# A new plan for the first part of a packed-attention, gated-unit and leaky-ReLU kernel

## The chip, the core and the metric

The kernel runs on one core of a Trainium2 chip. The metric is the time of one execution on the device in microseconds, as the median of several runs. One more execution was taken with the hardware profiler; every row shown here is from that one.

## The reference, cut to what matters

```
p_packed = sm_attn(p, k, v)            # 8 batches x 8 heads: 32 packed queries over 576 keys, head dim 64
out      = sm_attn(q, p_packed, p_packed)        # 576 queries over the 32 packed keys
x = out.transpose(0, 2, 1, 3).reshape(4608, 512)
x = (sigmoid(x @ w_gate) * (x @ w_val)) @ w_out          # w_gate, w_val: 512 x 1536
h = x @ w_in                                             # 512 x 2048
return max(0.01 * h, h) @ w_out2
```

The weights arrive as float64 in pairs of 32-bit words, and the kernel itself turns them into float32.

## The kernel before, in words

There are two parts. The **first part** runs batch by batch (b = 0 to 7). Of each batch it computes the two attentions and then the gated products for 12 blocks f of 128 columns, and stores each block in DRAM (`g1d`). Beside this it converts the weights. The **second part** multiplies by the three remaining weight matrices (line 851) in blocks of 768 tokens, with fewer products by a scheme of sums and differences. It begins when the last gated block is stored.

A `Plan` writes the order of the work out before anything runs on the chip. Every task has an engine (PE, ACT, DVE, POOL or DMA), a cost in us, a rank, tasks that it comes after, and buffers that it takes from named pools and gives back. `Plan.run` steps through a list schedule: whenever an engine is free in the plan, the ready task of lowest rank whose buffers are free is placed next on that engine. On the chip every engine then takes its instructions in that order and waits on semaphores. A task that the plan thinks ready and that isn't holds up all that stands behind it on its engine. A result counts as there 0.1 us after its task, a load 2.2 us after.

The tasks of the first part:

- **Weight units** (`unit`): a load of 512 KB on the SP queue into one of four `raw64` buffers, two ACT passes (lines 227, 234), two DVE passes (lines 238, 242), one addition on POOL (line 249). There are 24 units for gate and value weights (`unit_gv`, four for each of six column groups i, ranks -60 + 4i and up). There are 44 more for the later weights (`staged`, ranks from 900), which are then combined on POOL (line 310), split (ACT line 316, POOL line 322) and stored in DRAM from POOL's queue (line 330).
- **Attention** (`attention(b)`, base rank 100 (b - 1)): loads of k, p, v and q; transposes of k (DVE lines 410 to 416); first scores (`scores1`, PE line 427, both head groups G in one task); row maximum (`max1`), exponential (`exp1`), normalisation, a transposition on PE (`flip`, line 482) and its copy (`unflip`), the product with v (`pv`, line 503), the packing (`pack1` to `pack3`); then transposes of q, second scores (line 427), softmax on DVE in four steps around `exp2` (ACT line 547), and the split of the result into the high and low operands Ah and Al (`fin`, ACT line 578 and DVE line 580). The two halves h of the second attention are tasks of their own, as are the two groups G of the first.
- **Combinations** (`m_mm`, PE line 658): for each i the packed rows times the gate and value weights, then split by ACT (line 672, `mh`) and DVE (line 675, `ml`).
- **Gated products** (`mm`, PE line 691): for each f two tasks of 12 matmuls, gate and value; a sigmoid on ACT (`gate`, line 701), a multiplication on DVE (`times`, line 707) and a store on the SP queue.

PSUM holds four tiles. The plan has them as two pools: `pair` with two for the gated products, and `misc` with two for everything else. Batch 0's loads have ranks -100 to -56.5, in front of and among the first gate and value units; batch 1's have ranks from 0, behind all of them. Combinations have ranks 100 b + 16 i - 95, sigmoids and multiplications 100 b + 8 f - 90.

Of the kernel before, what the change touches and what calls it, by code (L numbers as in the profile page):

```python
# [29 lines left out]
class Plan:  # L30
# [7 lines left out]
    LAG = {"DMA": 2.2}  # L38

    def __init__(self):  # L40
        self.tasks, self.pools, self.holders = [], {}, {}
# [4 lines left out]
    def add(self, engine, us, rank, fn, after=(), take=(), give=()):  # L46
        i = len(self.tasks)
        self.tasks.append((engine, us, rank, fn, [a for a in after if a is not None], take, give))
        for name in dict.fromkeys(name for name, _ in take):
            self.pools[name][1].append(i)  # L50
        for key in give:
            self.holders[key] = self.holders.get(key, 0) + 1
        return i

    def run(self):
# [12 lines left out]
        while len(order) < n:  # L68
            for e, heap in ready.items():
# [3 lines left out]
                while heap:  # L73
# [3 lines left out]
                    if all(  # L77
# [9 lines left out]
                        us = self.tasks[i][1]  # L87
# [4 lines left out]
                        heapq.heappush(events, (now + us + self.LAG.get(e, 0.1), i))  # L92
# [12 lines left out]
            while events and events[0][0] <= now:  # L105
                _, i = heapq.heappop(events)
                if i < 0:
                    continue
                for j in next_of[i]:
# [23 lines left out]
def pack_attention_glu_lrelu(  # L133
# [83 lines left out]
    def unit(key, rank, load, target, after=(), give=(), loads=1):  # L217
# [148 lines left out]

    def attention(b):
        st = {}
# [52 lines left out]
        def scores(ps, w, key, half):  # L421

            for e in range(2):
                for j in range(NJ):
                    for G in range(2):
# [9 lines left out]
        def scores1():  # L435
            ps = st["sk"] = [ps_pair() for _ in range(2)]
            for half in range(2):
                scores(lambda G, j: ps[G][rows(G, j), half, :HS], pt, "k", half)
# [7 lines left out]
        def max1(G):  # L446
            def fn():
                mx = small("mx", [P, 1])
                nc.vector.tensor_reduce(out=mx, in_=st["sk"][G][:, :, :HS], axis=AX.XY, op=ALU.max)
# [4 lines left out]
        def exp1(G):  # L454
            def fn():
                a, sm = big(), small("sm", [P, 1])
                nc.scalar.activation(
                    a.rearrange("p (x y) -> p x y", x=2), st["sk"][G][:, :, :HS], AF.Exp,
# [110 lines left out]
        def fin(half, part):  # L569
            def fn():  # L570
# [14 lines left out]
        ld = r0 if b else -100  # L585
        Lk = [add("DMA", 1.8, ld + G, load_qk(k, "k", G), take=[K("qk", "k", G)]) for G in range(2)]
        Lp = add("DMA", 0.7, ld + 0.5, load_p, take=[K("praw")])
        Lv = add("DMA", 3.6, ld + 2 if b else -58.5, load_v, take=[K("v")])
        Lq = [add("DMA", 1.8, (ld + 3 if b else -57.5) + G, load_qk(q, "q", G), take=[K("qk", "q", G)])
              for G in range(2)]  # L590
        tp = add("DVE", 0.25, r0, p_t, [Lp] + ([packed[b - 1, "ck"]] if b else []), give=[K("praw")[1]])
        tk = [
            add("DVE", 0.75, r0 + 0.1 * j, tr("k", j), [Lk[j // 2]], take=[K("w576", "tk", j)],
                give=[K("qk", "k", j // 2)[1]])
            for j in range(NJ)
        ]
        ck = add("PE", 2.3, r0 + 1, scores1, [tp, *tk], take=[K("misc", "sk", 0), K("misc", "sk", 1)],
                 give=[K("w576", "tk", j)[1] for j in range(NJ)])
        packed[b, "ck"] = ck
        ex, fl, un = [], [], []  # L600
        for G in range(2):
            m = add("DVE", 0.95, r0 + 2 + G, max1(G), [ck])
            ex.append(add("ACT", 0.9, r0 + 2 + G, exp1(G), [m], take=[K("w576", "a", G)],
                          give=[K("misc", "sk", G)[1]]))
        for G in range(2):
            nm = add("DVE", 0.2, r0 + 4 + G, norm1(G), [ex[G]])
            nm = add("ACT", act(576), r0 + 4 + G, scale1(G), [nm])
            fl.append(add("PE", 0.7, r0 + 4 + G, flip(G), [nm], take=[K("misc", "f", G)],
                          give=[K("w576", "a", G)[1]]))
            un.append(add("ACT", 1.0, r0 + 5 + G, unflip(G), [fl[G]], take=[K("aT", G)],  # L610
                          give=[K("misc", "f", G)[1]]))
        pvt = add("PE", 2.1, r0 + 7, pv, [*un, Lv], take=[K("misc", "pp")],
                  give=[K("aT", 0)[1], K("aT", 1)[1], K("v")[1]])
        p1 = add("DVE", 0.5, r0 + 7, pack1, [pvt])
        p2 = add("PE", 0.2, r0 + 7, pack2, [p1])
        p3 = add("DVE", 0.25, r0 + 7, pack3, [p2], take=[K("pps")], give=[K("misc", "pp")[1]])
        packed[b] = p3
        tq = [
            add("DVE", 0.75, r0 + 8 + 0.1 * j, tr("q", j), [Lq[j // 2]], take=[K("w576", "tq", j)],
# [3 lines left out]
        last = []  # L623
        for h in range(2):
            c = add("PE", 1.2, r0 + 9 + h, scores2(h), [p3, *tq], take=[K("misc", "sq", h)],
                    give=[K("w576", "tq", j)[1] for j in range(NJ)])
            a = add("DVE", 0.8, r0 + 9 + h, soft2a(h), [c], take=[K("w576", "t", h)],
                    give=[K("misc", "sq", h)[1]])
            a = add("DVE", 1.7, r0 + 9 + h, soft2b(h), [a])
            last.append(add("ACT", 0.8, r0 + 9 + h, exp2(h), [a]))  # L630
        begin = add("", 0, r0 + 9, lambda: None, take=[K("A")])
        fins = []
        for h in range(2):
            a = add("DVE", 1.7, r0 + 11 + h, soft2c(h), [last[h]])
            a = add("DVE", 0.8, r0 + 11 + h, soft2d(h), [a], take=[K("w576", "u", h)],
                    give=[K("w576", "t", h)[1]])
            a = add("ACT", act(576), r0 + 11 + h, fin(h, 0), [a, begin])
            fins.append(add("DVE", dve(576), r0 + 11 + h, fin(h, 1), [a],
                            give=[K("w576", "u", h)[1]]))
        ready_a[b] = fins  # L640

# [3 lines left out]
    def gated(b, units):  # L645
# [70 lines left out]
        for i in range(NF1 // 2):  # L716
            m = add("PE", 1.2, r0 + 16 * i - 95, m_mm(i), [packed[b], *units[i]], take=[K("misc", i), K("mhl", i)],
                    give=[("pps", b)])
            h = add("ACT", act(1024), r0 + 16 * i - 95, m_split(i, 0), [m])
            l = add("DVE", dve(1024), r0 + 16 * i - 95, m_split(i, 1), [h], give=[K("misc", i)[1]])  # L720
            for f in (2 * i, 2 * i + 1):
                r = r0 + 8 * f
                g = add("PE", 1.6, r, mm(f, 0), [l, *ready_a[b]], take=[K("pair", f, 0)])
                vv = add("PE", 1.6, r + 1, mm(f, 1), [g], take=[K("pair", f, 1)],
                         give=[K("mhl", i)[1]] + ([("A", b)] if f == NF1 - 1 else []))
                s = add("ACT", act(576), r - 90, gate(f), [g], take=[K("sg", f)], give=[K("pair", f, 0)[1]])
                if b == B - 1 and f == NF1 - 1:
                    x = add("DVE", dve(576), r - 90, lambda: (times(NF1 - 1)(), store(NF1 - 1)()),
                            [s, vv], give=[K("pair", f, 1)[1], K("sg", f)[1]])
                    g1_done[b].append(x)  # L730
                    glu_end[b] = x
                else:
                    x = add("DVE", dve(576), r - 90, times(f), [s, vv], give=[K("pair", f, 1)[1]])
                    g1_done[b].append(add("DMA", 0.95, r - 90, store(f), [x], give=[K("sg", f)[1]]))
# [310 lines left out]
    with tc.manual_schedule():  # L1045
# [6 lines left out]
        attention(0)  # L1052
        for b in range(B):
            if b + 1 < B:
                attention(b + 1)
            gated(b, units)
# [40 lines left out]
```

## Time and profile before

| what | us |
|---|---|
| median of 3 runs (1528.1 to 1539.04) | 1528.98 |
| the profiled execution's own time | 1533.33 |
| its span, first to last instruction | 1531.6 |
| last gated matmul ends, first matmul of line 851 at full flow | 554.8 and 559.8 |

PE is TensorE's matmuls, PEld its weight loads, DVE VectorE, ACT ScalarE, POOL GpSimd, SP the engine whose queue issues most loads and stores (SPq). In the tables of stretches each engine's busy time stands with its instructions in brackets, then the mean granted TensorE clock as a share of full speed, the mean busy share of the DMA engines and what they moved. In lists of waits the columns are the time in total, how often, and the longest.

### The profile page before, as it was taken

The page shows a single profiled execution, that of the slowest core. Times are in us where ns is not written, and L with a number is a line of the kernel's source. Part 1 is how long each engine was busy: PE and PEld are TensorE (multiplying, and loading weights), DVE is VectorE, ACT ScalarE, POOL GpSimd, SP SyncE. Part 2 cuts the span into 40 slices and gives each one's busy share as a digit, 9 for nine tenths or more (in the row PEclk, how much of TensorE's full clock was granted, in tenths as well). Part 3 has the DMA queues.
Part 4 walks back from the last instruction along what each step waited for, and adds up shares of the span by engine and source line. Part 5 has one row for each costly group of instructions (what it writes and reads, how often), then busy time and mean ns, then how long its engine had stood idle before and what let it go on. Part 6 is the DMA issues. An engine that isn't in the chain of part 4 may idle for free.

```text
span 1531.6 us, 26682 instructions
## 1 busy us (share of the span) xinstructions
PE 1424.7 (93%) x10368; PEld 1335.4 (87%) x10368; DVE 1066.6 (70%) x1350; ACT 763.9 (50%) x1015; POOL 491.6 (32%) x571
## 2 busy tenths in 40 slices
PE   4586889889889989999999999999999999999997
PEld 1464767778767889999999999999999999999997
DVE  4788787889886447578467856686558854985483
ACT  4476766767666334454245434544355434543450
POOL 1347486396767201003510250026001620040002
PEclk8698999999989999999999999999999999999999
DMA  9997888788875739888988898889988998897886
GB/s 223 227 275 237 287 262 308 251 268 296 283 250 208 283 104 336 295 252 274 351 297 255 262 367 292 254 264 328 333 252 264 285 359 270 253 298 250 253 253 179
DMA packets 150829, 414.92 MB, mean 271 GB/s; under 512 B 32800, under 2 KB 43504, under 8 KB 150704
## 3 DMA queue, kind: packets, MB, share of 16 engines
q1 hardware_dynamic: 121056, 335.71, 69.5%
q0 software_dynamic: 26208, 77.09, 14.3%
q8 instruction: 83, 1.36, 0.3%
q10 hardware_dynamic: 3440, 0.42, 0.2%
q14 instruction: 42, 0.34, 0.1%
HBM read 335.02 MB, written 78.12 MB: 270 GB/s over the span
## 4 chain that ended last, share of the span: by engine, by line
PE 80%; DMA 8%; DVE 4%; ACT 4%; issue 2%; SPq 1%; POOL 1%; POOLq 0%; ACTq 0%; DVEq 0%
PE ps_pair L851 62%; PE ps_pair L691 14%; DMA raw<-in_moe_w_gate_dram 2%; PE ps_pair L658 2%; DMA raw<-in_moe_w_in_dram 1%; DMA raw<-in_moe_w_val_dram 1%; PE ps_pair L427 1%; DMA wd<-HL 1%; DVE ml L675 1%; ACT L701 1%; DMA raw<-in_moe_w_out_dram 1%; DVE Y L242 1%; DVE sg L707 1%; PE ps_pair L503 1%; ACT mh L672 0%
## 5 line engine op out<-in xcount | busy, mean ns | idle before, releaser
L851 PE MATMUL ps_pair<-op,wu 128*128 128x384 f32 x5544 | 964.0, 337 | 4.3 <-ACT op L794 4.0
L851 PEld LDWEIGHTS ps_pair<-op,wu 128*128 128x128 f32 x5544 | 963.0, 188 | 5.2 <-ACT op L794 4.2
L1031 POOL DMA_DIRECT2D out_dram<-os x225 | 132.3, 596 | 628.6 <-DVE os L1013 537.3
L794 ACT CAST op<-rawg 128x768 fp32r<-128x768 f32 x168 | 137.7, 835 | 211.9 <-DVE rawg L785 104.4
L691 PE MATMUL ps_pair<-Ah,ml 128*128 128x288 f32 x768 | 180.6, 317 | 55.6 <-ACT Ah L578 24.9
L691 PEld LDWEIGHTS ps_pair<-Ah,ml 128*128 128x128 f32 x768 | 127.0, 197 | 104.3 <-ACT sg L701 30.4
L799 DVE TENSOR_TENSOR op<-rawg,op 128x768 fp32r<-128x768 f32 x168 | 158.3, 952 | 75.4 <-ACT op L794 74.0
L868 DVE TENSOR_TENSOR tmp<-ps_pair,tmp 128x768 f32<-128x768 f32 x72 | 68.9, 957 | 152.9 <-PE ps_pair L851 104.4
L691 PE MATMUL ps_pair<-Al,mh 128*128 128x288 f32 x768 | 170.2, 303 | 1.1 <-DVE Al L580 1.1
L691 PE MATMUL ps_pair<-Ah,mh 128*128 128x288 f32 x768 | 169.1, 302 | 0.0
L794 ACT CAST op<-G 128x768 fp32r<-128x768 f32 x168 | 134.6, 834 | 59.9 <-PE ps_pair L851 44.8
L799 DVE TENSOR_TENSOR op<-G,op 128x768 fp32r<-128x768 f32 x168 | 156.0, 951 | 7.7 <-ACT op L794 7.3
L924 POOL DMA_DIRECT2D rawg<-g1d x96 | 68.7, 719 | 208.0 <-DVE op L799 95.1
L691 PEld LDWEIGHTS ps_pair<-Al,mh 128*128 128x128 f32 x768 | 128.9, 197 | 1.8 <-DVE Al L580 1.8
L691 PEld LDWEIGHTS ps_pair<-Ah,mh 128*128 128x128 f32 x768 | 128.1, 196 | 0.0
L987 ACT ACTIVATE G<-G 128x768 f32<-128x768 f32 x96 | 81.2, 846 | 59.1 <-DVE G L984 58.1
L322 POOL TENSOR_TENSOR HL<-Y,HL 128x1024 fp32r<-128x1024 f32 (+1 forms) x44 | 94.3, 2147 | 43.1 <-ACT HL L316 42.9
L701 ACT ACTIVATE sg<-ps_pair 128x576 f32<-128x576 f32 x96 | 62.4, 650 | 83.0 <-PE ps_pair L691 77.7
L862 ACT COPY tmp<-ps_pair 128x768 f32<-128x768 f32 x72 | 57.7, 802 | 91.0 <-PE ps_pair L851 90.5
L707 DVE TENSOR_TENSOR sg<-sg,ps_pair 128x576 f32<-128x576 f32 x96 | 71.3, 743 | 42.6 <-ACT sg L701 17.8
L785 DVE TENSOR_TENSOR rawg<-rawg 128x768 f32<-128x768 f32 x96 | 90.3, 954 | 5.2 <-DMA rawg<-g1d 2.9
L785 DVE TENSOR_TENSOR G<-G 128x768 f32<-128x768 f32 x96 | 91.4, 953 | 0.3
(78 smaller groups left out, 1196.0 us busy)
## 6 DMA issues: line engine op xcount, KB each, us to landing
wu<-wu SPq DMA_DIRECT2D x168, 512.0 KB, 4.7
wu<-wd SPq DMA_DIRECT2D x168, 512.0 KB, 4.5
wu<-wp SPq DMA_DIRECT2D x126, 512.0 KB, 4.8
g1d<-sg SPq DMA_DIRECT2D x96, 288.0 KB, 4.0
rawg<-g1d POOLq DMA_DIRECT2D x48, 384.0 KB, 8.0
raw<-in_moe_w_out_dram SPq DMA_DIRECT2D x28, 512.0 KB, 5.3
raw<-in_k_dram SPq DMA_DIRECT2D x16, 576.0 KB, 5.6
raw<-in_q_dram SPq DMA_DIRECT2D x16, 576.0 KB, 5.6
```

Source lines behind the costliest of these rows:

```text
L322: nc.gpsimd.tensor_tensor(out=hl[:, :, 1], in0=t["y"][:, x0:x1], in1=hl[:, :, 0].bitcast(F32), op=ALU.subtract,)
L691: nc.tensor.matmul(ps[:, t, :HS], w, x[:, t * HS:(t + 1) * HS], start=(n == 0), stop=(n == len(pairs) - 1),)
L701: nc.scalar.activation(st["sg", f], st["gv", f, 0][:, :, :HS], AF.Sigmoid)
L707: nc.vector.tensor_tensor(out=sg, in0=sg, in1=st["gv", f, 1][:, :, :HS], op=ALU.mult)
L785: nc.vector.tensor_tensor(out=src(g, o), in0=src(g, a), in1=src(g, b), op=ALU.subtract)
L794: nc.scalar.copy(h, src(g, c))
L799: (nc.gpsimd if on_pool(i, g) else nc.vector).tensor_tensor(out=l, in0=src(g, c), in1=tiles["op", st, i, g][0].bitcast(F32), op=ALU.subtract)
L851: nc.tensor.matmul(ps[c][:, m, :TB], a, x[:, kk, :], start=(fresh and kk == 0 and y == 0), stop=(end and kk == 1 and y == 2), skip_group_c ...
L868: nc.vector.tensor_tensor(out=T[x], in0=ps[c][:, :, :TB], in1=T[y], op=ALU.add)
L924: nc.gpsimd.dma_start(out=t[:, :, t0 - base:t0 - base + m], in_=g1d[b][:, f:f + 2, s0:s0 + m])
L987: nc.scalar.activation(dest(), dest(), AF.Prelu, alpha=0.01)
L1031: queues[turn % len(queues)].dma_start(out=ob[:, s0:s0 + m, d0:d0 + 32], in_=tiles["os", c][32 * y:32 * y + 32, x, t0:t0 + m],)
```

## The change: what it does

- **The planner.** A task on another engine counts as ready 0.5 us after what it waits for (`SLACK`; 0.2 us for tasks of attention, added by `late`), on the same engine at once. A load counts as there 3.5 us after its cost. ACT's tasks can name a function table, and a switch of table costs 1.5 us in the plan.
- **Costs.** Loads of weight units 1.7 becomes 2.15 us (gate and value) or 1.8; the DVE passes 0.6 and 0.78 become 0.45 and 0.7 (gate and value) or 0.85 and 0.9; loads of batches 0 and 1 become 2.5 (k, q) and 5.5 (v).
- **PSUM.** The pools `pair` and `misc` become one pool `ps` of four.
- **Ranks.** Batch 1's k and p load at -55, v at -49, q at -39, among the gate and value units. Attention's first half has base r0 - 60 (r0 - 80 for batch 0), its middle r0 - 30; batch 1's r0 is 20 lower. Sigmoids and multiplications go from -90 to -100, combinations from -95 to -60, `exp2` to r0 - 100.
- **Tasks.** `scores1` is one task for each G. Both `exp1` are one ACT task, and so are both `exp2`; the pair comes after both of what either needs. The tasks are added in another order (`attention` yields three times).

```diff
-    LAG = {"DMA": 2.2}
+    SLACK = 0.5
...
-                        us = self.tasks[i][1]
+                        us, table = self.tasks[i][1], self.tasks[i][7]
+                        if table and table != self.table:
+                            self.table, us = table, us + 1.5
...
-                        heapq.heappush(events, (now + us + self.LAG.get(e, 0.1), i))
+                        heapq.heappush(events, (now + us + (3.5 if e == "DMA" else 0), i))
...
-                        heapq.heappush(ready[self.tasks[j][0]], (self.tasks[j][2], j))
+                        wait = 0 if self.tasks[j][0] == self.tasks[i][0] else self.tasks[j][8]
+                        heapq.heappush(events, (now + wait, n + j))
...
-        L = add("DMA", 1.7, rank, do_load, take=[("raw64", ("raw64", key))])
+        L = add("DMA", 2.15 if rank < 0 else 1.8, rank, do_load, take=[("raw64", ("raw64", key))])
...
-        s = add("DVE", 0.6, rank, shift, [a])
-        s = add("DVE", 0.78, rank, sign, [s], give=[("raw64", key)])
+        s = add("DVE", 0.45 if rank < 0 else 0.85, rank, shift, [a])
+        s = add("DVE", 0.7 if rank < 0 else 0.9, rank, sign, [s], give=[("raw64", key)])
...
-                    ("A", 2), ("pps", 2), ("pair", 2), ("mhl", 2), ("sg", 3)):
+                    ("A", 2), ("pps", 2), ("mhl", 2), ("sg", 3)):
...
-    plan.pool("misc", 2, loose=True)
+    plan.pool("ps", 4, loose=True)
...
+    def late(engine, *args, **more):
+        return add(engine, *args, slack=0.2, **more)
...
-        ld = r0 if b else -100
+        r1 = r0 - (60 if b else 80)
+        ld = (-100, -55)[b] if b < 2 else r1
...
+        for G in range(2):
+            ck.append(late(
+                "PE", 1.15, r1 + 1 + G, scores1(G), [tp, *tk[2 * G:2 * G + 2]], take=[K("ps", "sk", G)],
+                give=[K("w576", "tk", 2 * G + e)[1] for e in range(2)],
+            ))
+            mx.append(late("DVE", 0.95, r1 + 2 + G, max1(G), [ck[G]]))
...
+        ex = late("ACT", 1.5, r1, lambda: (exp1(0)(), exp1(1)()), mx,
+                  take=[K("w576", "a", G) for G in range(2)],
+                  give=[K("ps", "sk", G)[1] for G in range(2)], table="exp")
+        yield
+        r0 -= 20 * (b == 1)
...
+        Lv = add("DMA", 5.5 if b < 2 else 4.5, (-58.5, -49)[b] if b < 2 else r1 + 2, load_v, take=[K("v")])
+        Lq = [add("DMA", 2.5 if b < 2 else 2.0, ((-57.5, -39)[b] if b < 2 else r1 + 3) + G, load_qk(q, "q", G), take=[K("qk", "q", G)])
...
-            last.append(add("ACT", 0.8, r0 + 9 + h, exp2(h), [a]))
+        ex = late("ACT", 1.5, r0 - 100, lambda: (exp2(0)(), exp2(1)()), sb, table="exp")
...
-            m = add("PE", 1.2, r0 + 16 * i - 95, m_mm(i), [packed[b], *units[i]], take=[K("misc", i), K("mhl", i)],
+            m = add("PE", 1.2, r0 + 16 * i - 60, m_mm(i), [packed[b], *units[i]], take=[K("ps", i), K("mhl", i)],
...
-                s = add("ACT", act(576), r - 90, gate(f), [g], take=[K("sg", f)], give=[K("pair", f, 0)[1]])
+                s = add("ACT", act(576), r - 100, gate(f), [g], take=[K("sg", f)], give=[K("ps", f, 0)[1]],
+                        table="sigmoid")
```

## Rows read from the trace of the kernel before

**Rows 1.** Busy time of each engine by stretches of the first part.

```profile
0.00:50.00 50.00, 17.39 (x236) 7.33 (x236) 27.32 (x55) 19.92 (x35) 7.09 (x11) 0.75 1.03 223
50.00:100.00 50.00, 38.03 (x308) 31.07 (x309) 36.60 (x63) 29.80 (x47) 24.43 (x18) 0.81 0.97 260
100.00:150.00 50.00, 35.03 (x421) 27.89 (x422) 45.36 (x67) 32.68 (x48) 30.16 (x26) 0.86 0.75 240
150.00:500.00 350.00, 315.75 (x3413) 258.12 (x3412) 282.86 (x413) 237.20 (x333) 233.85 (x204) 0.96 0.81 268
500.00:555.00 55.00, 54.53 (x452) 48.03 (x450) 21.31 (x26) 15.87 (x21) 8.02 (x12) 1.00 0.59 213
```

**Rows 2.** The gated matmuls (line 691) alone, PE and PEld, over that part.

```profile
0.00:555.00 555.00, 345.57 (x2304) 323.50 (x2304) 0.92 0.81 255
```

**Rows 3.** The chain that ended last, in order of time: start, length, what.

```profile
35.19 9.31 DMA raw<-in_moe_w_gate_dram
...
519.78 1.02 PE ps_pair L658 x16
520.80 6.54 PE ps_pair L691 x48
```

**Rows 4.** Two of the page's costliest groups: second part's matmuls, sigmoids.

```profile
L851 PE MATMUL ps_pair<-op,wu 128*128 128x384 f32 x5544 | 964.0, 337 | 4.3 <-ACT op L794 4.0
...
L701 ACT ACTIVATE sg<-ps_pair 128x576 f32<-128x576 f32 x96 | 62.4, 650 | 83.0 <-PE ps_pair L691 77.7
```

**Rows 5.** Who waited for whom, 0 to 100 us.

```profile
ACT wc L227 <- DMA raw<-in_moe_w_gate_dram: 28.4, 10, 9.2
...
PE ps_pair L691 <- ACT Ah L578: 13.5, 1, 13.5
...
ACT wc L227 <- DMA raw<-in_moe_w_val_dram: 12.7, 7, 3.7
```

**Rows 6.** PE's waits, 100 to 150 us.

```profile
PE ps_pair L691 <- ACT Ah L578: 11.4, 2, 7.2
```

**Rows 7.** PE's waits, 150 to 500 us.

```profile
PE ps_pair L691 <- ACT sg L701: 10.3, 7, 4.2
PE ps_pair L691 <- DVE ml L675: 6.8, 5, 3.0
PE ps_pair L482 <- ACT w L474: 6.4, 5, 2.1
```

**Rows 8.** SP's queue in order of time, 0 to 140 us.

```profile
44.87 3.25 SPq L381 DMA_DIRECT2D raw<-in_q_dram  x2
...
84.08 2.61 SPq L266 DMA_DIRECT2D raw<-in_moe_w_gate_dram  x4
...
89.20 1.84 SPq L266 DMA_DIRECT2D raw<-in_moe_w_val_dram  x2
```

**Rows 9.** ACT's instructions in order of time, 0 to 145 us.

```profile
48.63 1.33 ACT L578 CAST Ah<-w 128x576 fp32r<-128x576 f32 x2 [2.81 <-DVE w L565]
...
98.67 0.67 ACT L227 ACTIVATE wc<-raw 128x512 f32<-128x512 f32 x1
```

**Rows 10.** DVE's instructions in order of time, 0 to 145 us.

```profile
49.48 1.42 DVE L580 TENSOR_TENSOR Al<-w,Ah 128x576 fp32r<-128x576 f32 x2
...
103.93 2.75 DVE L410 STREAM_TRANSPOSE w<-raw 128x576 f32<-128x576 f32 x4
...
131.99 3.58 DVE L580 TENSOR_TENSOR Al<-w,Ah 128x576 fp32r<-128x576 f32 x1
...
138.04 1.79 DVE L580 TENSOR_TENSOR Al<-w,Ah 128x576 fp32r<-128x576 f32 x1
```

**Rows 11.** POOL's instructions in order of time, from two stretches.

```profile
132.62 2.33 POOL L322 TENSOR_TENSOR HL<-Y,HL 128x1024 fp32r<-128x1024 f32 x1
...
489.83 0.77 POOL L330 DMA_DIRECT2D wd<-HL  x1 [0.30 <-POOL HL L322]
```

**Rows 12.** Loads of the sigmoid's table on ACT, whole first part.

```profile
L701 ACT ACT_TABLE_LOAD x22 | 28.2, 1283 | 0.4
```

More of the change, by code (lines that the diff above doesn't have):

```diff
@@ L30, with add @@
 class Plan:
-    LAG = {"DMA": 2.2}
+    SLACK = 0.5
     def __init__(self):
-        self.tasks, self.pools, self.holders = [], {}, {}
+        self.tasks, self.pools, self.holders, self.table = [], {}, {}, None
     def pool(self, name, n, loose=False):
         self.pools[name] = [n, [], 0, loose]
-    def add(self, engine, us, rank, fn, after=(), take=(), give=()):
+    def add(self, engine, us, rank, fn, after=(), take=(), give=(), table=None, slack=None):
         i = len(self.tasks)
-        self.tasks.append((engine, us, rank, fn, [a for a in after if a is not None], take, give))
+        self.tasks.append((engine, us, rank, fn, list(after), take, give, table,
+                           slack or self.SLACK))
         for name in dict.fromkeys(name for name, _ in take):
@@ L108, in run @@
                     continue
+                if i >= n:
+                    j = i - n
+                    heapq.heappush(ready[self.tasks[j][0]], (self.tasks[j][2], j))
+                    continue
                 for j in next_of[i]:
@@ L419, in tr, with scores @@
             return fn
-        def scores(ps, w, key, half):
+        def scores(ps, w, key, half, groups=(0, 1)):
             for e in range(2):
                 for j in range(NJ):
-                    for G in range(2):
+                    for G in groups:
                         r = slice(32 * j, 32 * j + 32)
@@ L433, in scores, with scores1, fn @@
                         )
[L435 to L438, printed above, removed]
+        def scores1(G):
+            def fn():
+                ps = st["sk", G] = ps_pair()
+                for half in range(2):
+                    scores(lambda g, j: ps[rows(g, j), half, :HS], pt, "k", half, (G,))
+            return fn
         def scores2(half):
@@ new lines, in attention @@
+        yield
+        r0 -= 20 * (b == 1)
+        fl, un = [], []
+        for G in range(2):
+            nm = late("DVE", 0.3, r0 - 30 + G, norm1(G), [ex])
+            nm = late("ACT", 0.8, r0 - 30 + G, scale1(G), [nm])
+            fl.append(late("PE", 0.8, r0 - 30 + G, flip(G), [nm], take=[K("ps", "f", G)],
+                          give=[K("w576", "a", G)[1]]))
+            un.append(late("ACT", 0.9, r0 - 29 + G, unflip(G), [fl[G]], take=[K("aT", G)],
+                          give=[K("ps", "f", G)[1]]))
@@ L613, in attention @@
+        Lv = add("DMA", 5.5 if b < 2 else 4.5, (-58.5, -49)[b] if b < 2 else r1 + 2, load_v, take=[K("v")])
+        Lq = [add("DMA", 2.5 if b < 2 else 2.0, ((-57.5, -39)[b] if b < 2 else r1 + 3) + G, load_qk(q, "q", G), take=[K("qk", "q", G)])
+              for G in range(2)]
+        pvt = late("PE", 2.1, r0 - 27, pv, [*un, Lv], take=[K("ps", "pp")],
                   give=[K("aT", 0)[1], K("aT", 1)[1], K("v")[1]])
-        p1 = add("DVE", 0.5, r0 + 7, pack1, [pvt])
-        p2 = add("PE", 0.2, r0 + 7, pack2, [p1])
@@ L732, in gated @@
                 else:
[L733 to L734 removed]
+                    x = add("DVE", dve(576), r - 100, times(f), [s, vv], give=[K("ps", f, 1)[1]])
+                    g1_done[b].append(add("DMA", 0.95, r - 100, store(f), [x], give=[K("sg", f)[1]]))
     NWU, NOP = 6, 22
@@ L1051, in pack_attention_glu_lrelu @@
         units = [[unit_gv(i, g, jh) for g in range(2) for jh in range(2)] for i in range(NF1 // 2)]
[L1052 to L1056, printed above, removed]
+        steps = [attention(b) for b in range(B)]
+        for b in range(B + 1):
+            if b < B:
+                next(steps[b])
+            if b:
+                next(steps[b - 1])
+            if b < B:
+                next(steps[b])
+            if b:
+                gated(b - 1, units)
         rank = 900.0
```

65 lines of the change are left out of this document (27 added, 38 removed).

## The prediction

> **What bounds the kernel now.** I read the table of stretches first, because the change touches only what happens before the last gated block is stored. In the first 555 us PE stands idle for 94 (each stretch less its busy time): 32.6 in the first 50 us, 12.0 in the next, 15.0 in the third, 34.2 from 150 to 500, and then half a microsecond [rows 1]. In the same stretches the granted clock is 0.75, 0.81, 0.86, 0.96 and 1.00: wherever PE had stood idle, part of its work then ran at the lower of its two levels, 1.2 instead of 2.4 GHz. The cost shows in the gated matmuls: 2304 of them took 345.6 us [rows 2], while 48 at full speed take 6.54 [rows 3], which makes 314 for all. So the low clock costs a further 31 us there. Idle time and low clock together are the 125 us that a plan can win back in the first part; no engine's amount of work changes.
>
> The last 55 us are plain matmul, 54.5 of 55 busy, so the first part ends where PE's queue ends, and a microsecond taken out of an earlier idle stretch moves that end, as long as the weights are ready. They have slack: POOL issues its last store of converted weights at 489.8 [rows 11], 65 us ahead. The other engines are no tighter than PE: from 150 to 500 us DVE is busy 283 of 350, ACT 237, POOL 234, DMA 0.81 [rows 1]. DVE at 81% is the nearest rival. The second part is matmul throughout: 5544 matmuls with 4.3 us of idle time in front of all of them [rows 4].
>
> Then the lists of waits, to see what the idle time is. In the first 100 us ACT stands 41.1 us at the head of its queue for gate and value weights (28.4 + 12.7) [rows 5], with attention's work behind it; the chain of waits agrees, with a gate load of 9.3 us in it [rows 3]. DMA is saturated there, share 1.03 and 0.97 at 223 and 260 GB/s [rows 1]. PE waits 13.5 us for batch 0's Ah [rows 5] and then 11.4 for batch 1's [rows 6]. Later the waits are short and many: sigmoids 10.3, the split of the combinations 6.8, the flip's input 6.4 [rows 7].
>
> **The change part by part. Batch 0's attention.** Its loads keep their ranks, so its last q arrives as now. What changes is that the plan no longer believes in weights that haven't come: a load of 512 KB at 223 GB/s takes 2.35 us against 1.7 planned before and 2.15 now. ACT's exponentials and casts then stand ahead of the conversions that would hold them. But one task for both exponentials makes the first half wait for the second. I take Ah from 48.6 [rows 9] to about 46, a gain of 2 to 3, with bounds 0 and 5.
>
> **Batch 1's loads.** They don't simply come earlier. Batch 1's q was issued at 44.9 and 48 in the old order, long before the last gate and value units at 84 to 91 [rows 8], because the unit loads were waiting for `raw64` buffers. Rank -39 now puts q behind 22 of the 24 units, so it moves *back* to about 85. In exchange the units of column groups 2 to 4 move forward by what v and q took, 2.5 MB or 10 us at 242 GB/s, the mean of the two stretches. The total is the same, so all of it is in at about 95, as now: units 12.6 MB, two batches 7.4, eight gated stores 2.4, together 22.4 MB or 93 us at 242. The last unit was converted at 98.7 [rows 9].
>
> Batch 0's gated products need 7.56 us of PE for each i (1.02 + 6.54) [rows 3], against 9.4 us of DMA for its four units at 223 GB/s. So from 46 on they follow the loads. With groups 2 to 4 earlier and the last group converted near 100, I get 100 + 4 for conversion and split + 7.6, or 112.
>
> **Batch 1's operands.** From the transposes of q at 103.9 to the last Al at 139.8 the old chain takes 36 us [rows 10]; its own instructions, about 30 between these two, sum to some 21 by their durations in the same view and in PE's. The difference is queueing, and POOL. With q landing near 95, the bounds are 95 + 21 = 116 and 95 + 36 = 131. I take 28 us, the middle, hence 123. All of batch 0's products are done by then, and batch 1's start at 123 instead of 139.9: a gain of 17, with bounds 9 and 24. The gain at Ah of batch 0 lies inside this and isn't added.
>
> **PSUM, slack, ranks, from 150 on.** With two tiles the gated products can be one task ahead of the sigmoid, with four up to three ahead whenever attention holds none: that is aimed at the 10.3 us of sigmoid waits. A slack of 0.5 us moves dependent tasks back in the queues, aimed at the 13.2 of splits and flips. The clock adds to each of them: 0.96 over 350 us. Exponentials in pairs allow 16 changes to the exponential's table and back, against 22 loads of the sigmoid's table now [rows 12]: 6 pairs of loads at 1.28 us, 15 us of ACT, which is off the path (237 of 350 busy). The trace of before has no pool of four, so I bound it: nothing at all, or even a loss of 10 (the PSUM rival below, at a quarter of its price), on one side; on the other nearly all of the 34 us idle, 30. I take 13, a little over a third, because DVE leaves little room  (283 of 337 us are 84%) and its stalls are as below.
>
> One row speaks against flat prices for DVE: two subtractions into Al take 1.42 us together at 49.5, and one takes 3.58 at 132.0 [rows 10]. The latter ends 0.6 us after POOL's own operation, which runs from 132.62 to 134.95 [rows 11]. The new prices of 0.85, 0.9, 2.0 and 2.3 can be right in the mean and wrong by nearly 3 us for one instruction, so queues laid out by them will still stall.
>
> The Trainium skill, "SBUF — State Buffer", section "Who interferes with whom", gives this as a rule: the ports that VectorE shares with GpSimd are an exclusive lock for a whole instruction, and a VectorE instruction with two SBUF inputs contends with a GpSimd one that reads SBUF. The trace agrees, with 3.58 us against 0.71. If the rule decided every late stall, the 13 us of the later part would be nothing, and the sum 1529 - 17 = 1512 in place of 1499.
>
> **What is costed at nothing.** The second part gets the new slack too, so ACT's and DVE's orders there can change. PE's order is fixed by the ranks of its products, and it never waits in the trace; bounds -2 and +5. The weights' cover of 65 us holds for a first part shorter by 30. SP's queue passes batch 1's loads ahead of units that wait for a buffer; what is behind them waits at most for the 1.2 us of issue of a unit.
>
> **The sum.** 17 + 13 = 30 us off the profiled execution's 1533.3 gives 1503; that execution lies 4.35 above the median, so the forecast is 1499.
>
> **The rivals.** *DVE and POOL keep the stalls.* The first part's waits only move: batch 1's chain takes its old 36 us, a gain of 9, and after 150 nothing is won. For it: DVE at 45.4 of 50 between 100 and 150 [rows 1], and the locked instructions. Against it: PE's waits there are few and long. It gives 1529 - 10 = 1519.
>
> *The shared pool starves the gated products (slower).* Attention and combinations of the next batch now rank ahead of the products and may take three of the four tiles, where two were safe from them. With one tile, a product of 12 matmuls (1.64 us) is followed by its sigmoid (0.65 us [rows 4]) or a multiplication of like length, with the hand-over an estimated 0.9 us in which PE has nothing: 35% of that time. It loses the 17 us of the start if PE is on one tile for 14% of 350 us. At a third (117 us) it costs 41, and the time is 1529 + 41 - 17 = 1553. For it: scores hold two tiles through maxima and both exponentials now, and the combination's tile waits for DVE. Against it: the list schedule counts the tiles and can place a product in between.
>
> *The later stalls mostly vanish.* Start 22, later 28 with the clock: 1529 - 50 = 1479. For it: clock and idle time feed each other. Against it: DVE would be above 88%.
>
> *The ranks do nothing,* since SP waits for `raw64` in the same places: this gives the first rival's time and is counted there.
>
> **How the numbers follow.** Forecast 0.46, first rival 0.26, PSUM 0.10, later stalls 0.18. One per cent (15 us) is about what a measurement of this kernel can tell. Faster by more than that, below 1514: nearly all of the forecast, all of the last rival, a fifth of the first, 0.66. Slower by more: most of the PSUM rival, 0.09. The rest 0.25. For the range I take the start's 24 and later 30 together as the far end, 1475, and 1472 with the second part's 2; above it reaches over the first rival to 1529, so that the PSUM rival and a little beside are left out.
>
> **What would show it.** Right: batch 0's products end near 112, batch 1's begin near 123, the last gated matmul ends near 525; the second part lasts 972 us as now. The waits of ACT for gate and value weights fall below 25 us; some 16 loads of the sigmoid's table; sigmoid waits on PE below 5 us. Wrong: if batch 1's Ah still comes after 131, if new waits of line 691 for tiles appear from 150 on, or if the weights' last store moves behind the last gated matmul.

## The result and the profile after

The changed kernel takes 1506.73 us (median of 4 runs, 1502.66 to 1508.25) against 1529.84 for the kernel before in the same sitting (4 runs, 1528.1 to 1539.04). The ratio is 0.984 with a 95% interval of 0.9812 to 0.9868, which is 20 to 29 us less (24.5 by the ratio itself). The profiled execution of after took 1502.66 us, with a span of 1500.9; it is the fastest of the four. Against the profiled execution of before, 1533.33, that is 30.7 us less. Every row below is from such profiled executions, so the rows have 6 to 8 us more to explain than the medians.

First the stretches, as in [rows 1]: length, PE, PEld, DVE, ACT, POOL, granted clock, DMA share, GB/s.

```profile
0.00:50.00 50.00, 25.18 (x299) 10.61 (x299) 30.32 (x65) 18.58 (x33) 7.06 (x11) 0.68 1.01 228
50.00:100.00 50.00, 42.91 (x443) 33.51 (x443) 49.02 (x77) 36.47 (x60) 21.15 (x16) 0.91 1.02 246
100.00:150.00 50.00, 41.44 (x468) 33.47 (x469) 43.22 (x65) 31.11 (x48) 22.98 (x20) 0.93 0.87 282
150.00:500.00 350.00, 329.40 (x3428) 268.60 (x3427) 306.70 (x405) 221.85 (x319) 244.15 (x203) 0.99 0.78 268
500.00:530.00 30.00, 25.55 (x197) 22.91 (x196) 12.80 (x15) 9.91 (x14) 12.71 (x18) 0.95 0.92 318
```

Up to 150 us PE stands idle for 40.5 us instead of 59.6, from 150 to 500 for 20.6 instead of 34.2, and the clock rises with it, from 0.96 to 0.99 in the long stretch. Busy time at half clock counts double, so it doesn't measure progress. A better measure: count the matmuls of each line in a stretch and charge each at its cost at full clock (gated 6.54 us for 48, combinations 1.02 for 16 [rows 3], scores 2.10 for 64, product with v 1.66 for 80, packing 0.27 each, and for 10 flips an estimate of 1.42; they took 1.1 to 1.3 where the clock was full). A matmul on the edge of a slice counts on both sides, so an entry can be up to 0.7 us too high. By 150 us PE has then done 71.1 us of work before and 86.5 after; from 150 to 500 us 299.1 and 314.3. So the start gives **15.4 us** and the later part **15.2 us**.

The chain that ended last (start, length, what) shows the end of the first part and the beginning of the second.

```profile
510.52 12.90 PE ps_pair L718 x96
...
523.51 0.77 DVE sg L734
...
528.55 202.20 PE ps_pair L879 x1151
```

The last gated matmul ends at 523.4 instead of 554.8, and line 879 (851 before) is at full flow at 528.55 instead of 559.8. From there to the end of the span it is 972.4 us, against 1531.6 - 559.8 = 971.8 before. The whole gain lies ahead of the second part, which is what it was [rows 4]:

```profile
L879 PE MATMUL ps_pair<-op,wu 128*128 128x384 f32 x5544 | 964.4, 337 | 4.6 <-ACT op L822 4.1
```

Then the waits (who for whom: total, times, longest). ACT's for gate and value weights, 0 to 100 us, as in [rows 5]:

```profile
ACT wc L235 <- DMA raw<-in_moe_w_gate_dram: 23.4, 8, 8.4
ACT wc L235 <- DMA raw<-in_moe_w_val_dram: 9.1, 5, 3.3
```

PE's from 150 to 500 us, as in [rows 7]:

```profile
PE ps_pair L718 <- DVE sg L734: 10.0, 5, 3.4
PE ps_pair L685 <- DVE sg L734: 3.7, 3, 2.6
PE ps_pair L718 <- ACT sg L728: 2.7, 4, 1.3
```

The three groups of before, 23.5 us together, have shrunk to 2.7 for the sigmoid, nothing of the products for `ml`, 1.9 for the flips (which now wait for the combinations' split and no longer for ACT's `w`). In their place stands one that was small before: 13.7 us for DVE's multiplication (line 734), which frees the value product's PSUM tile. Before, it was

```profile
PE ps_pair L658 <- DVE sg L707: 2.2, 3, 1.2
```

Ahead of 150 us, the 24.9 us for Ah [rows 5, 6] are 3.3, all for batch 0; the longest between 100 and 150 is now 7.2 for `ml`.

ACT's and DVE's timelines (start, length, engine, line, what) show the operands of batches 0 and 1:

```profile
50.81 1.33 ACT L593 CAST Ah<-w 128x576 fp32r<-128x576 f32 x2 [0.60 <-DVE w L580]
...
119.47 0.67 ACT L593 CAST Ah<-w 128x576 fp32r<-128x576 f32 x1
```

```profile
121.27 0.74 DVE L595 TENSOR_TENSOR Al<-w,Ah 128x576 fp32r<-128x576 f32 x1
```

Batch 1's last Al is there at 122.0, 17.8 us earlier than the end of the one at 138.04 [rows 10]. Batch 0's Ah is *later* than before (50.81 against 48.63 [rows 9]).

Last, the 23 us in which batch 1's products begin, cut out of the third stretch (columns as in the stretches above), before and then after:

```profile
127.00:150.00 23.00, 11.36 (x110) 9.62 (x111) 20.56 (x31) 11.88 (x17) 15.05 (x14) 0.70 0.61 210
```

```profile
127.00:150.00 23.00, 21.24 (x299) 16.95 (x299) 22.20 (x29) 15.84 (x23) 17.95 (x17) 1.00 0.90 291
```

PE's timelines show the first products of batch 1 at full flow, before and then after:

```profile
137.95 0.61 PE L691 MATMUL ps_pair<-Ah,ml 128*128 128x288 f32 x1 [7.23 <-ACT Ah L578]
...
139.89 0.61 PE L691 MATMUL ps_pair<-Al,mh 128*128 128x288 f32 x1 [1.09 <-DVE Al L580]
```

```profile
129.65 0.53 PE L718 MATMUL ps_pair<-Ah,ml 128*128 128x288 f32 x2
```

By 127 us both kernels have ended batch 0's products, and the new one is only some 3 us of work ahead. In the next 23 us it does some 21 us of work, the old one 8. So most of the start's gain falls here, where PE was waiting for batch 1's operands and then ran at a granted clock of 0.70.

### The profile page after: what moved, and what is told of

Same layout as the page of the kernel before. It is cut to its first block, busy times and chain, and to the rows that moved or that the text cites. A ratio compares the mean times of both kernels' runs of the same rounds, so it can differ in the third digit from the quotient of the medians.

```text
span 1500.9 us, 26560 instructions
## 1 busy us (share of the span) xinstructions
PE 1426.7 (95%) x10368; PEld 1330.8 (89%) x10368; DVE 1091.6 (73%) x1350; ACT 738.3 (49%) x999; POOL 496.4 (33%) x571
## 3 DMA queue, kind: packets, MB, share of 16 engines
q1 hardware_dynamic: 121056, 335.71, 71.1%
## 4 chain that ended last, share of the span: by engine, by line
PE 71%; DVE 3%; issue 1%; ACT 0%; DMA 0%; POOL 0%; POOLq 0%; DVEq 0%; ACTq 0%
PE ps_pair L879 64%; PE ps_pair L718 6%; PE ps_pair L685 1%; DVE sg L734 1%; PE ps_pair L440 0%; DVE ml L702 0%; DVE Y L250 0%; DVE Y L246 0%; DVE w L572 0%; DVE w L425 0%; DMA g1d<-sg 0%; POOL out_dram L1059 0%; DVE w L543 0%; DVE mx L553 0%; DVE sm L569 0%
## 5 line engine op out<-in xcount | busy, mean ns | idle before, releaser
L822 ACT CAST op<-rawg 128x768 fp32r<-128x768 f32 x168 | 132.3, 834 | 184.0 <-DVE rawg L813 142.5
L718 PE MATMUL ps_pair<-Ah,ml 128*128 128x288 f32 x768 | 174.8, 309 | 26.0 <-DVE sg L734 11.7
L827 DVE TENSOR_TENSOR op<-rawg,op 128x768 fp32r<-128x768 f32 x168 | 155.2, 951 | 37.9 <-ACT op L822 37.1
L718 PEld LDWEIGHTS ps_pair<-Ah,ml 128*128 128x128 f32 x768 | 123.7, 192 | 60.8 <-DVE sg L734 20.9
L718 PE MATMUL ps_pair<-Al,mh 128*128 128x288 f32 x768 | 167.1, 299 | 1.1 <-DVE Al L595 1.1
L718 PEld LDWEIGHTS ps_pair<-Al,mh 128*128 128x128 f32 x768 | 125.4, 192 | 1.7 <-DVE Al L595 1.7
L330 POOL TENSOR_TENSOR HL<-Y,HL 128x1024 fp32r<-128x1024 f32 (+1 forms) x44 | 98.7, 2252 | 40.7 <-ACT HL L324 40.7
L728 ACT ACTIVATE sg<-ps_pair 128x576 f32<-128x576 f32 x96 | 62.2, 650 | 82.4 <-PE ps_pair L718 75.7
```

The source lines that it names most:

```text
L330: nc.gpsimd.tensor_tensor(out=hl[:, :, 1], in0=t["y"][:, x0:x1], in1=hl[:, :, 0].bitcast(F32), op=ALU.subtract,)
L718: nc.tensor.matmul(ps[:, t, :HS], w, x[:, t * HS:(t + 1) * HS], start=(n == 0), stop=(n == len(pairs) - 1),)
L728: nc.scalar.activation(st["sg", f], st["gv", f, 0][:, :, :HS], AF.Sigmoid)
L822: nc.scalar.copy(h, src(g, c))
L827: (nc.gpsimd if on_pool(i, g) else nc.vector).tensor_tensor(out=l, in0=src(g, c), in1=tiles["op", st, i, g][0].bitcast(F32), op=ALU.subtract)
```

## The experiments

Each ratio is against the kernel before on the same chip; where nothing else is said a kernel is the changed one with the edit shown. What an edit costs is told as the difference of its median from 1506.73; the ratios, which allow for the chip, give the same to within 3.5 us. The last two columns are the measure of work explained above, up to 150 us and from 150 to 500, from each profile.

| kernel | us | ratio (95%) | by 150 | 150 to 500 |
|---|---|---|---|---|
| before | 1529.84 | | 71.1 | 299.1 |
| after | 1506.73 | 0.984 (0.9812 to 0.9868) | 86.5 | 314.3 |
| old_ranks1 | 1502.77 | 0.9824 (0.9787 to 0.986) | 85.4 | 314.0 |
| old_load_prices | 1541.61 | 1.008 (1.0053 to 1.0108) | 83.5 | 286.5 |
| old_lag | 1537.14 | 1.0031 (1.001 to 1.0053) | 92.0 | 277.6 |
| lag_stores_only | 1507.72 | 0.9869 (0.9834 to 0.9905) | 92.6 | 305.3 |
| lag_stores_50 | 1509.77 | 0.9879 (0.9846 to 0.9913) | 85.6 | 316.0 |
| before_lag35 | 1520.72 | 0.9938 (0.9914 to 0.9963) | 77.0 | 299.9 |
| old_att_ranks | 1537.25 | 1.0037 (1.0019 to 1.0055) | 85.4 | 278.7 |
| single_exps | 1524.07 | 0.9956 (0.9934 to 0.9977) | 82.4 | 298.8 |
| two_pools | 1518.85 | 0.9921 (0.9901 to 0.9942) | 84.1 | 296.6 |
| no_slack | 1516.17 | 0.9906 (0.9872 to 0.9939) | 83.1 | 313.0 |
| slack_06 | 1513.73 | 0.9879 (0.9842 to 0.9916) | 87.5 | 309.6 |
| after_no_shift | 1494.62 | 0.9755 (0.9705 to 0.9804) | 87.6 | 321.1 |

**Batch 1's loads back at their old ranks.**

```diff
-        ld = (-100, -55)[b] if b < 2 else r1      # v: (-58.5, -49), q: (-57.5, -39)
+        ld = (-100, 0)[b] if b < 2 else r1        # v: (-58.5, 2),   q: (-57.5, 3)
-        r0 -= 20 * (b == 1)
```

> The changed kernel with batch 1's loads back at ranks 0 to 4 and its attention 20 ranks later; all else as changed. Theory 1: SP waits for raw64 buffers anyway, so batch 1's loads go out between the units as before, and the time stays within 5 us of 1507, with Al of batch 1 by 127. Rival (these ranks win the start): batch 1's products begin at 135 to 140 as in the kernel before, and the time is 1520 to 1525.

The time is that of after within the scatter. In SP's queue batch 1's q is issued here at

```profile
44.69 0.83 SPq L394 DMA_DIRECT2D raw<-in_q_dram  x2
```

and in after at

```profile
41.51 1.51 SPq L394 DMA_DIRECT2D raw<-in_q_dram  x2
```

so the new ranks move it by 3 us, forward. The part of the change with the most numbers in it moves the end by nothing that these runs can tell.

**The loads' prices and the lag back to the old ones.**

```diff
-    2.15 if rank < 0 else 1.8          (weight units)
+    1.7
-    2.5 and 5.5 for batches 0 and 1, 2.0 and 4.5 after   (k and q, v)
+    1.8 and 3.6
-    (3.5 if e == "DMA" else 0)
+    (2.2 if e == "DMA" else 0)
```

> The changed kernel with the old prices of loads alone (1.7 us a weight unit, 1.8 k and q, 3.6 v, 2.2 us until a load counts as there); ranks, pool, slack and pairs as changed. Theory 1 (the start is won because attention no longer stands behind loads that haven't come): ACT's waits for gate and value weights go back from 32 to about 40 us in the first 100, batch 1's last Al comes 8 to 15 us later than 122, and the time is 1515 to 1522. Rival (batch 1's ranks win the start): Al stays near 122, time 1507. Rival (any new plan moves the time by some 5 us by chance): the time moves without its share showing before 150 us.

The whole gain is gone and more, but not at the start: 83.5 of 86.5 us of work are still done by 150 us. The loss is behind it, where PE waits 18.5 us for sigmoids. The signs of theory 1 are half there: ACT's waits for gate and value weights are back at 39.6 us (32.5 in after), and batch 1's last Al is ready at 129.7, 7.7 us later than in after. Of the work done by 150 us this takes only 3 us.

**The lag alone.** Only the last of those edits, 3.5 back to 2.2. The lag belongs to every DMA task of the plan, to stores as well as to the loads that the text on the change and the expectations speak of.

> The changed kernel with one number undone: a load counts as there 2.2 us after its cost, in place of 3.5; the prices of loads stay new. Theory 4 (the old load prices cost 35 us mainly by this lag, since after 150 us the prices differ by 0.1 to 0.9 us and the lag by 1.3 for each load): 1525 to 1540, with 15 us and more of PE's waits for sigmoids from 150 to 500. Rival (the prices of the first loads do it): 1507 to 1512.

This alone costs 30 us. PE's waits from 150 to 500 us:

```profile
PE ps_pair L718 <- ACT sg L728: 23.9, 7, 9.5
PE ps_pair L685 <- ACT sg L728: 8.8, 3, 6.2
```

What ACT waits for, 100 to 540 us:

```profile
ACT HL L324 <- DMA wu<-HL: 46.5, 12, 6.8
...
ACT HL L324 <- DMA wp<-HL: 18.1, 6, 5.3
ACT HL L324 <- DMA wd<-HL: 12.6, 7, 4.0
```

ACT's timeline in front of the longest of PE's waits, and then PE's:

```profile
338.45 1.04 ACT L324 CAST HL<-Y 128x1024 fp32r<-128x1024 f32 x1 [1.74 <-DMA wu<-HL]
345.69 0.83 ACT L324 CAST HL<-Y 128x768 fp32r<-128x768 f32 x1 [6.19 <-DMA wu<-HL]
346.54 1.28 ACT L728 ACT_TABLE_LOAD   x1
347.83 1.19 ACT L728 ACTIVATE sg<-ps_pair 128x576 f32<-128x576 f32 x2
```

```profile
338.62 0.43 PE L718 MATMUL ps_pair<-Ah,mh 128*128 128x288 f32 x2
348.53 0.85 PE L718 MATMUL ps_pair<-Ah,ml 128*128 128x288 f32 x2 [9.49 <-ACT sg L728]
```

This is a mechanism that the prediction doesn't have. The converted weights are cast into one of two `HL` buffers (line 324), which a *store* has to empty first. The cast's rank is 900 - 2000, ahead of every sigmoid, so the plan places it as soon as it believes a buffer free. It reckons a store of 768 columns at 768/340 + 2.2 = 4.5 us; the DMA issues of this kernel (count, KB each, median us from issue to landing) give for `wu`

```profile
wu<-HL POOLq DMA_DIRECT2D x8, 768.0 KB, 7.9
```

The cast stands at the head of ACT for 77.2 us in all (46.5 + 18.1 + 12.6). Not all of this reaches PE: between 260 and 273 us ACT stands 10.0 us at two casts, and PE waits 1.4. But of PE's 32.7 us for sigmoids (23.9 + 8.8), 28.1 end within 3 us after the start of a cast that had waited for a store. With 3.5 the same three waits are 10.4 + 8.2 + 6.9 = 25.5 us in after.

**3.5 for stores, 2.2 for loads; then 5.0 for stores.**

```diff
-    (3.5 if e == "DMA" else 0)
+    ((2.2 if self.tasks[i][5] else 3.5) if e == "DMA" else 0)      # loads take a buffer, stores don't
```

> The changed kernel with the lag of 3.5 us kept for stores and 2.2 us again for loads. Theory 7 (the lag works through the stores of the converted weights: with 2.2 us the plan puts ACT's cast into an HL buffer whose store hasn't landed, and sigmoids stand behind it): ACT's waits for those stores stay under 40 us between 100 and 540, PE's waits for sigmoids from 150 to 500 under 14 us, and the time is 1503 to 1515. Rival (it works through the loads): 1528 to 1540, with ACT waiting for loads of weights.

> The changed kernel with a lag of 5 us for stores and 3.5 for loads. Theory 7 carried further: ACT's waits for the stores fall from 25 to under 12 us, and the time is 1495 to 1507, the best version so far if it is below 1500. Rival (the converted weights come later by this, and the second part waits for them): 1510 to 1520.

The first puts nearly all of it back, 1507.72 us, with 28.2 us of waits at the cast (13.3 + 9.4 + 5.5). So the lag acts through the stores; that is shown. The edit covers the gated blocks' stores too; that those of the converted weights matter is read from the waits, since in old_lag ACT's sigmoids wait for the gated ones only 1.1 us. The second doesn't carry on from there: the waits stay at 25.8 us, where less than 12 were expected. It ends the gated matmuls at 522.5, a microsecond sooner than after, and gives it back at the start of the second part, where its weights aren't in (PE's timeline):

```profile
532.62 42.64 PE L879 MATMUL ps_pair<-op,wu 128*128 128x384 f32 x231 [10.16 <-DMA wu<-wp]
```

**The lag put into the kernel before.**

```diff
-    LAG = {"DMA": 2.2}
+    LAG = {"DMA": 3.5}
```

> The kernel before with 3.5 us in place of 2.2 until a load or store counts as done, and nothing else. If the lag alone carries the gain: 1505 to 1515. If the parts only work together (undoing the lag costs 30 us, undoing attention's ranks 30, and the whole change gives 24): within 7 us of 1531, since the kernel before has late stalls of other kinds too and its start is untouched.

It gains 9.5 us alone, outside the 7 of "only together" and short of 1505 to 1515. Its waits at the cast fall from 35.8 to 19.5 us, but by the table this brings hardly anything: of the work gained 5.9 us lie before 150 us and 0.8 behind it. What it doesn't mend are the waits of the old plan, in this list of PE's from 0 to 150 us:

```profile
PE ps_pair L691 <- ACT Ah L578: 17.0, 3, 12.2
PE ps_pair L482 <- ACT w L474: 7.7, 3, 3.8
```

So the kernel before had less to lose at `HL` (35.8 us), and the new plan, with the old lag, much (77.2 us). What makes the difference between these two wasn't tried; neither was a third `HL` buffer, for which SBUF has no room as the other buffers are laid out.

**Attention back at its old ranks.**

```diff
-        r1 = r0 - (60 if b else 80)                # middle: r0 - 30 to r0 - 27; exp2: r0 - 100
-        r0 -= 20 * (b == 1)
+        r1 = r0                                    # middle: r0 + 4 to r0 + 7;   exp2: r0 + 9
```

> The changed kernel with attention's ranks as in the kernel before (first half at r0, middle from r0 + 4, second exponentials at r0 + 9, batch 1 without its 20); the first loads' ranks, pool, slack, prices and pairs as changed. Theory 5 (attention placed ahead of combinations and products wins the start, since batch 1's Ah came at 115 to 125 in all four runs so far and at 137 before): batch 1's second Ah at 130 or later, and the time 1517 to 1525. Rival (the planner's timing wins it): Ah by 122, time 1503 to 1510.

The loss, 30 us, came where it wasn't expected: batch 0's Ah comes at 62.01 and batch 1's at 124.95, yet 85.4 us of work are done by 150. From 150 to 500 us PE waits for attention itself:

```profile
PE ps_pair L717 <- ACT Ah L593: 12.3, 2, 8.8
PE ps_pair L497 <- ACT w L489: 11.5, 2, 6.2
PE ps_pair L684 <- DVE sg L733: 7.3, 1, 7.3
```

Batch 2's Ah starts at 196.76, and in after at 171.03. Giving attention's first half, its middle and `exp2` ranks that are 34 to 109 lower, where a batch is 100, is thus worth as much here as the lag.

**One exponential for each task, as before.**

```diff
-        ex = late("ACT", 1.5, r1, lambda: (exp1(0)(), exp1(1)()), mx, ...
+        ex = [late("ACT", 0.75, r1, exp1(G), [mx[G]], ...) for G in range(2)]      # exp2 likewise
```

> The changed kernel with the two exponentials of each attention as tasks of their own again, each after its own inputs. Theory (the pairs matter little, since ACT is off the path): within 7 us of 1507, with some 4 more loads of tables. Rival (table loads between the exponentials delay sigmoids): 1515 to 1525.

It costs 17 us, as the rival said. The loads of the sigmoid's table on ACT (count, busy time, mean ns, idle before), here and then in after:

```profile
L730 ACT ACT_TABLE_LOAD x24 | 30.8, 1283 | 0.4
```

```profile
L728 ACT ACT_TABLE_LOAD x14 | 18.0, 1283 | 0.2
```

With the exponential's own tables that is 47 loads against 27, 20 times 1.28 = 25.7 us of ACT. PE's waits for sigmoids from 150 to 500 us are 15.7 us here (11.5 + 3.2 + 1.0), against 2.7, and a load of the sigmoid's table begins 2 us before the end of each of the seven. So, with ACT busy for 241 of these 350 us, the loads aren't off the path. What they cost by themselves isn't shown: the edit also changes the order, and ahead of some of these waits ACT stood at the cast too.

**PSUM in two pools of two; slack 0.1, and 0.6.**

```diff
-    plan.pool("ps", 4, loose=True)
+    plan.pool("pair", 2)                            # gated products
+    plan.pool("misc", 2, loose=True)                # all else
...                                                 # each task takes its tile from its own pool again
```

```diff
-                        wait = 0 if ... else self.tasks[j][8]
+                        wait = 0.1                  # no_slack; slack_06 has SLACK = 0.6 instead
```

> The changed kernel with two PSUM tiles reserved for the gated products and two for the rest, as in the kernel before. Theory 2 (the later 13 us come from the shared pool): PE's waits for sigmoids from 150 to 500 go back from 2.7 to about 10 us, and the time is 1512 to 1518. Rival (DVE sets the late waits whatever the tiles): within 3 us of 1507. Rival (sharing starves the products): faster than 1503.

> The changed kernel with 0.1 us between dependent tasks everywhere, in place of 0.5 and 0.2. Theory 3 (the slack removes waits for splits and flips): PE's waits of these two kinds from 150 to 500 rise from under 2 to some 10 us, and the time is 1511 to 1516. Rival (it only reorders): within 3 us of 1507.

> The changed kernel with a slack of 0.6 us in place of 0.5, which nothing on the chip asks for: a measure of what any new plan does by chance. If the parts undone so far (12 and 9 us) are more than chance, the time is within 5 us of 1507. If it is 1515 or more, or 1498 or less, single undone parts of that size tell little.

Two pools cost 12 us, nearly all behind 150 us (17.7 us of work there, 2.4 before, in a profiled execution 5.5 us above the median), but the sigmoid waits that this was aimed at don't reach the 10 expected: 4.7 us, with 9.1 for the multiplication and 5.5 for the packing. Without slack the kernel loses 9 us, and again not by the waits expected (3.1 us for `ml`, none for flips): the gated matmuls end at 529.4, 6 us later, and then the second part waits for weights.

```profile
539.72 10.10 PE L879 MATMUL ps_pair<-op,wu 128*128 128x384 f32 x48 [10.32 <-DMA wu<-wp]
```

A slack of 0.6 instead of 0.5, a change with no meaning of its own, costs 7 us (from the medians; 6 by the ratios, whose intervals overlap). It falls between the two outcomes that its expectation names. I take 7 us as the scale of chance, since any edit of the plan deals all queues anew, but it is one sample, and chance may be larger. Against it 30 us are plain, 17 are more than twice it, 12 not quite twice, and 9 or less isn't one part's price. The same nudge moves PE's waits for sigmoids from 2.7 to 13.7 us.

**DVE relieved.** Leaves out the DVE shift pass of the 44 later weight units; the plan and its order stay, so this edit deals no queue anew.

```diff
-            nc.vector.tensor_single_scalar(x, x, 3, op=ALU.logical_shift_left)
+            if rank < 0:
+                nc.vector.tensor_single_scalar(x, x, 3, op=ALU.logical_shift_left)
```

> The changed kernel without the shift pass on DVE for the 44 later weight units (this part of the conversion is left out; the plan and every order stay as they are): some 42 us of DVE work less. Theory 6 (after the change DVE sets the late stalls): PE's waits for multiplications fall from 14 to under 6 us, and the time is 1490 to 1499. Rival (the order of the queues sets them): within 4 us of 1507.

Its stretch from 150 to 500 us:

```profile
150.00:500.00 350.00, 334.66 (x3488) 274.17 (x3487) 270.87 (x366) 223.75 (x322) 246.78 (x213) 0.99 0.81 274
```

and PE's waits there:

```profile
PE ps_pair L719 <- ACT sg L729: 11.7, 7, 2.6
PE ps_pair L719 <- DVE sg L735: 2.6, 2, 2.2
```

Both figures of theory 6 came. DVE falls from 307 to 271 us, and the kernel by 12. The waits for the multiplication fall from 13.7 to 2.8, and most of that appears again as waits for sigmoids. DVE sets part of what is left in after; behind it stands ACT.

## Why the prediction was right, and where its steps failed

**The sum held.** Of the two terms, 17 at the start measured 15.4 by the count of work, 13 from 150 on measured 15.2. They were 30 of the profiled execution's time, and 30.7 came. The median is 7.7 us above the forecast, because this took 4.35 off for a profiled execution above its median, and that of after lies 4.1 below its own: by all runs the change is worth 24.5 us (20 to 29), not 30. That both terms came out within 2 us is in part luck, since several of the steps below failed. Small slips in the working change nothing: v and q are 2.36 MB, not 2.5, two batches 7.2 and not 7.4, and the low end of the range is 1473.

**Batch 1's operands: right in time and in mechanism, wrong in what follows.** The last Al was put at 123 and ends at 122.0. Batch 1's products don't start there, though. Batch 0's products end at about 127 (126 before), not 112, with batch 1's and batch 2's attention set between them, and batch 1's start at 129.65: 10.2 us earlier than 139.89, not 17. The gap that was to close did close. Between 127 and 150 us PE is busy for 21.2 instead of 11.4 us, at a clock of 1.00 instead of 0.70, and this is some 12.7 of the start's 15.4 us. The clock, which the prediction doesn't count here, makes up for the later start.

**Batch 1's loads: the step failed.** q moves to 41.51, not back to 85. I read the ranks as SP's order; with four `raw64` buffers the next unit's load isn't ready in the plan when a buffer is missing, and a load of lower priority goes first, as before. That "the ranks do nothing" of the loads is shown by old_ranks1.

**Batch 0's Ah: failed.** 46 was said, 50.81 came; before, 48.63. ACT's waits for gate and value weights fell from 41.1 to 32.5 us, not below 25. The prices of the loads do act on these waits (39.6 us with the old prices and lag, 32.7 with the old lag alone), but they aren't what wins the start: with both old, 83.5 us of work are still done by 150.

**What brings batch 1's operands forward stays open.** In none of the ten edits of the new plan does the work by 150 us fall below 82.4. The lag alone in the kernel before raises it from 71.1 to 77.0. What no run undid is the new order of the tasks with its three steps, the ranks of sigmoids and combinations, the price of a table, DVE's prices and `scores1` in two. Or several parts each suffice.

**The later part: right in size, by other causes.** The pool and the slack were named as the means. Undone, two pools cost 12 us and the slack 9, near the scale of chance. The large parts are those that the prediction priced at the start or at nothing: the lag (30 us, through stores of weights, which it looks at only as the second part's supply), attention's ranks (30) and the pairs of exponentials (17), of which it said that their table loads are "off the path (237 of 350 busy)". These prices add to far more than the whole change: each part is worth this only beside the others, and the lag alone was worth 9.5 in the old plan.

**What would show it.** The sigmoid waits, 2.7 us, are below 5, but this sign says little: old_ranks1 has 10.8 at the products alone and the same time. Table loads of the sigmoid 14 (16 said), last gated matmul at 523.4 (525), second part 972.4 (972): right. Batch 0's products near 112, batch 1's near 123 and waits for weights below 25 us: wrong. Of the signs against it one did appear: 13.7 us in which products and combinations wait for tiles that the multiplication frees, against 2.2 before. The cover of weights held, if with less to spare than the last store suggests. In POOL's timeline this is at

```profile
494.93 0.76 POOL L338 DMA_DIRECT2D wd<-HL  x1 [0.30 <-POOL HL L330]
```

28 us ahead of the last gated matmul where it was 65, and two plans near this one already wait 10 us for weights at line 879.

**The rivals.** DVE and POOL keep the stalls (1519): refuted, though half of it is right, since the waits left in after are mostly DVE's. The shared pool starves the products (1553): refuted by two_pools, which is slower. The later stalls vanish (1479): no; PE still stands idle for 20.6 us there. DVE, named as what speaks against it, is already busy for 306.7 of 350 us.

## What to carry to other kernels

Where a plan sets the order, look for the task of highest priority that waits on something outside the engines, a buffer freed by a store, and set the plan's time for that transfer no shorter than its traced time (a further 1.5 us on top won nothing here): an in-order engine pays for a wrong belief with what stands behind it. An engine's free share says little of what a wait or a table load at the head of its queue costs. Before a part of such a change is given a price, nudge a constant that means nothing, to learn how much any new order moves the time.

## What the runs showed of the hardware

DVE's work grew while its instructions fell: 306.7 us for 405 between 150 and 500 us, against 282.9 for 413 [rows 1]. Two thirds of the growth sit in a pass that reads two tensors in SBUF (sign pass: count, busy us, mean ns), before and then after:

```profile
L242 DVE SCALAR_TENSOR_TENSOR Y<-raw,Y 128x512 int32<-128x512 int32 x37 | 39.4, 1081 | 0.2
```

```profile
L250 DVE SCALAR_TENSOR_TENSOR Y<-raw,Y 128x512 int32<-128x512 int32 x39 | 55.4, 1421 | 0.7
```

The shift pass, with one input, stays at 1.05 us (1.07 before), and one that reads PSUM, the multiplication, at 746 ns (742). POOL is busy for 244 us instead of 234 there. The Trainium skill, "SBUF — State Buffer", section "Who interferes with whom", has a VectorE instruction with two SBUF inputs contend with a GpSimd one that reads SBUF. The pattern agrees (1421 against 1081 ns), but no run here took POOL's work away, so the cause is argued and not shown. The second thing is the time until a store counts as done: 4.7 to 6.9 us in the median in after for 768 and 1024 KB from POOL's queue, up to 7.9 in old_lag. In both the smaller stores are no faster than the larger; in before two of the three kinds are.
